# A fused attention and gated-unit block: the first four token tiles centred only, their scale applied later, and the value weights loaded in four pieces from a second queue

## The chip, the core and the metric

The kernel runs on one NeuronCore of a Trainium2 chip. The core has five engines with queues of their own: PE (TensorE, matrix products; the profile lists its weight loads as PEld), DVE (VectorE), ACT (ScalarE), POOL (GpSimd) and SP, which here only issues DMAs. Each engine works through its queue in order, and semaphores order the engines among themselves. Sixteen DMA engines move the data. The metric is the device time of one execution in microseconds, as a median over runs: before the change 222.83 us (three runs, 222.78 to 222.85). The profile was taken in another execution, of 222.43 us.

## The reference, cut to what matters

```python
xn = layernorm(x)                       # (x - mean) / sqrt(var + 1e-5), 2048 tokens x 512
out = x + A(xn) + B(xn)

def A(x):                               # 32 heads of 16
    q, k, v = split(x @ wqkv)
    phi(u) = concat(softmax(u @ w_phi), softmax(-u @ w_phi))
    kv = phi(k)^T v ;  z = sum over tokens of phi(k)
    o = (phi(q) kv) / (phi(q) z + 1e-6)
    return o @ wo

def B(x):                               # 1792 wide
    return ((x @ w_gate) * (x @ w_up)) @ w_down
```

Everything that reads the normalised tokens xn is linear in them up to the softmax, and the gated unit is a product of two such terms.

## The kernel before, in words

The 2048 tokens are 16 tiles of 128. All tensors live in one SBUF array, `arena`, so the profile's names say `arena` for nearly everything and `ps` for PSUM; the line tells the groups apart.

*Layer norm.* `emit_ln_stats` takes the statistics of a tile (L410) and aggregates them (L412) on DVE, adds epsilon (L417, on DVE for tiles 0 to 3, on POOL for the later ones) and lets POOL raise it to the power of -1/2 (L419). `emit_xn` subtracts the mean and multiplies by the root in one DVE instruction (L434). Tiles 0 to 3 go one by one; PE transposes each by four products with an identity matrix (L442), and ACT copies the result out of PSUM into `xnT` (L443). The later tiles go in groups of four, and a DMA transpose, issued by SP, turns them.

*Products.* `k_pe` makes the values of a tile (four matmuls of 512 columns with the value weights; ACT copies them out at L507). `wprime` multiplies the transposed key or query weights with a block-diagonal form of w_phi, so that one product per tile gives the input of the softmax; the four block-diagonal tiles `wbd` are made by POOL in `make_wbd` (L392) once w_phi is there. `k_pk` and `q_pk` make the softmax inputs, and `emit_exp` writes them with both signs to SBUF (two ACT instructions out of PSUM, L467 and L468), takes the maximum on DVE and lets ACT make the exponentials. `glu` is one gated unit: two groups of four matmuls, an ACT copy of the gate and a DVE product (L545). `q_num` makes numerators and denominators of the attention and divides (L614, L615). `final` adds up the down projection of the gated units and the output projection in one PSUM bank; DVE adds x (L642), and SP stores the tile.

*Order.* Nothing of the order within an engine is written out by hand. Every step is recorded with what it reads and writes, a cost, and for a DMA a time `at` before which the planner does not believe it landed. `_order` then lays the steps out greedily engine by engine: the step that can start first, by priority among equals; steps marked `urgent` may go ahead of another. The costs and the `at` times change the order in which instructions stand in the queues, and nothing else: on the chip the semaphores decide. A line of the recording helpers therefore stands for many operations (all matmuls are L297, all ACT operations L277, plain DMAs L165, DMA transposes L164).

*The beginning.* SP issues the loads of x tiles 0, 1, 2-3, the value weights in one DMA, x 4-7, the first four of fourteen column tiles of the gate and up weights, w_phi, the key weights through a DMA transpose (L361), and then the rest of the gate and up weights. PE meanwhile runs 46 matmuls on zeros (L366).

Of the kernel before, what the change touches and what calls it, by code (L numbers as in the profile page):

```python
# [197 lines left out]
def _build(nc, es, A_x, A_wqkv, A_w_phi, A_wo, B_w_gate, B_w_up, B_w_down, out):  # L198
# [93 lines left out]
    def mms(items, prio=None, warm=False):  # L292

        def fn(e):
            ins = None
            for o, l, r, a, z in items:
                ins = e.matmul(o, lhsT=l, rhs=r, start=a, stop=z)  # L297
            return ins
        reads = []
        writes = []  # L300
        c = 0.0
        for o, l, r, a, z in items:
            reads += [l, r]
            writes.append(o)
            c += max(25.0, o.free_size() / 2.4 + 2.3) * (1.6 if warm else 1.0)
        return sc.step(PE, fn, reads=reads, writes=writes, cost=c, lat=260.0, prio=prio)
# [40 lines left out]
    def load_gu(on, f0, n, at):  # L347
# [3 lines left out]

    load_x(SP, 0, 1, 3150.0)
    load_x(SP, 1, 1, 3700.0)
    load_x(SP, 2, 2, 4800.0)
    load_w(SP, wv_v, A_wqkv[:, 1024:1536].rearrange("(q p) j -> p q j", p=128), 6800.0)
    load_x(SP, 4, 4, 8200.0)
    load_gu(SP, 0, 4, 10800.0)
    sc.dma(SP, wphi_v, bass.AP(tensor=A_w_phi.tensor, offset=A_w_phi.offset, ap=[[16, 128], [2048, NQ], [1, 16]]),
           at=12500.0)
    load_wT(1, 14500.0)  # L360
    load_gu(SP, 4, 10, 20500.0)  # L361


    zero = sbv("tree", 0, 128)
    dve(lambda e: e.memset(zero, 0.0), [], [zero], 128)  # L365
    mms([(bank(7, 0, 128), zero, zero, True, True)] * 46, warm=True)  # L366

# [37 lines left out]
    pool(lambda e: e.memset(mhalf, -0.5), [], [mhalf], 4)  # L405

    def emit_ln_stats(t0, n):
        ts = slice(t0, t0 + n)
        for t in range(t0, t0 + n):
            dve(lambda e, t=t: e.bn_stats(stats_v[:, t, 0:6], x_tile(t)), [x_tile(t)], [stats_v[:, t, 0:6]], 512)  # L410
        for t in range(t0, t0 + n):
# [3 lines left out]
        rstd4 = rstd_v[:, ts, 0:1]  # L415
        add = dve if t0 < 4 else pool
        add(lambda e: e.tensor_scalar(out=veps.unsqueeze(2), in0=var4, scalar1=1e-5, scalar2=None, op0=ALU.add),  # L417
            [mv_v[:, ts, :]], [veps], n)
        pool(lambda e: e.tensor_tensor(out=rstd4, in0=veps.unsqueeze(2), in1=mhalf[:, 0:n].unsqueeze(2), op=ALU.pow),  # L419
# [8 lines left out]
    def next_a():  # L428
        b = a_bank[0] % a_banks[0]
        a_bank[0] += 1  # L430
        return b

    def emit_xn(t):
        dve(lambda e: e.tensor_scalar(out=xn_tile(t), in0=x_tile(t), scalar1=mv_v[:, t, 0:1],  # L434
                                      scalar2=rstd_v[:, t, 0:1], op0=ALU.subtract, op1=ALU.mult),
            [x_tile(t), mv_v[:, t, 0:1], rstd_v[:, t, 0:1]], [xn_tile(t)], 512, rate=0.5)
        if t >= 4:
            sc.dma(SP, xnT_v[:, :, t * 128:(t + 1) * 128], xn_tile(t), transpose=True, issue=1250.0, land=3200.0,
                   at=36000.0 + 1300.0 * (t - 8) if t >= 8 else 22500.0 + 1300.0 * (t - 4))
            return  # L440
        b = next_a()
        mms([(bank(b, q * 128, 128), xn_tile(t)[:, q * 128:(q + 1) * 128], ident, True, True) for q in range(NQ)])  # L442
        act_op(xnT_v[:, :, t * 128:(t + 1) * 128], bank(b).rearrange("p (q s) -> p q s", q=NQ))  # L443

# [15 lines left out]

    def emit_exp(src_bank, e_out):

# [3 lines left out]
        tr = (i % 2) * 1024  # L466
        act_op(pst[:, 0:512], bank(src_bank))  # L467
        act_op(pst[:, 512:1024], bank(src_bank), scale=-1.0)  # L468
        src = pst.rearrange("p (g k) -> p g k", g=16)
# [34 lines left out]
    def k_pe(t):  # L504
        b = next_a()
        mms(group(bank(b), [(xnT(q, t * 128, 128), wv_v[:, q, :]) for q in range(NQ)]))
        act_op(vext_all[:, t, :, 0:64], bank(b).rearrange("p (c j) -> p c j", c=8))  # L507

    def k_pk(t):
        b = next_a()  # L510
        mms(group(bank(b), [(xnT(q, t * 128, 128), Wp_v[:, 1, q, :]) for q in range(NQ)]))
        p_slot["k", t] = emit_exp(b, ek_v[:, t, :])

# [73 lines left out]
    def q_pk(t):  # L587
        b = next_q()
        mms(group(bank(b), [(xnT(q, t * 128, 128), Wp_v[:, 0, q, :]) for q in range(NQ)]))
        p_slot["q", t] = emit_exp(b, eq(t))  # L590

# [17 lines left out]
    def q_num(t):  # L609
# [4 lines left out]
        dve(lambda e: e.reciprocal(out=w, in_=nd[:, :, 64:68]), [nd[:, :, 64:68]], [w], 32, rate=6.0)  # L614
        dve(lambda e: e.tensor_tensor(  # L615
            out=o.rearrange("p (g h d) -> p g h d", g=8, h=4),
            in0=nd[:, :, 0:64].rearrange("p g (h d) -> p g h d", h=4),
            in1=w[:, :, :, None].to_broadcast([128, 8, 4, 16]), op=ALU.mult),
            [nd[:, :, 0:64], w], [o], 512)

# [7 lines left out]
    def final(t, b, cols=(0, 512)):  # L628
# [12 lines left out]
        xs = x_tile(t)[:, c0:c1]  # L641
        dve(lambda e: e.tensor_tensor(out=og, in0=ob, in1=xs, op=ALU.add), [ob, xs], [og], c1 - c0, prio=-2.0)  # L642
        sc.dma(SP, out_flat[t * 128:(t + 1) * 128, c0:c1], og, is_out=True)
# [21 lines left out]

    for t in range(4):
        first = len(sc.steps)
        ln(t, 1)
        for st in sc.steps[first:]:
            st.urgent = True  # L670
        k_pe(t)
    make_wbd()
    wprime(1)
    for b0 in range(0, NT, 4):
# [5 lines left out]
        if b0 == 0:  # L680
            load_later(lambda: load_x(SP, 8, 8, 29000.0))
        if b0 == 4:
# [187 lines left out]
```

## Time and profile before

| | |
|---|---|
| median of three runs | 222.83 us |
| profiled execution | 222.43 us |
| its span, first to last instruction | 220.7 us |
| PE busy | 215.4 us, 98%, 1273 matmuls |
| DVE busy | 192.8 us, 87% |
| ACT busy | 114.4 us, 52% |
| POOL busy | 9.6 us, 4% |
| HBM read, written | 8.67 MB, 2.10 MB |

The profile gives busy times of the engines, groups of instructions by line, the chain of work that ended last (followed back from the last instruction, at each step to what released it), the DMA queues, and the time from the issue of a DMA to its landing. "<-" behind an instruction names what ended the idle time before it. Times count from the first instruction of the span. The ends of matmuls are modelled, so how fast PE works is read from the distance between starts. The row PEclk is the share of the clock that a throttle granted.

### The profile page before, as it was taken

Reading aid. Unit: us, or ns where it says so; the run is one execution under the profiler, and the core shown is the slowest. Engines: PE = TensorE matmul, PEld = TensorE weight load, DVE = VectorE, ACT = ScalarE, POOL = GpSimd, SP = SyncE. Lnnn points to the kernel's source line nnn. Section 1 sums busy time; section 2 is a strip of 40 time slices with the busy share of each in tenths; the row PEclk is TensorE's granted clock in tenths of the full one; section 3 lists DMA queues with packets and bytes.
Section 4 is the critical chain, followed back from the end, with each engine's and each line's share of the span. In section 5 each row is a group of like instructions: output and inputs, shape, how many; then the busy total and the mean of one; then the engine's idle time right before and its main releaser. Section 6 shows DMA issues by size and latency. Waiting matters only on the chain.

```text
span 220.7 us, 3555 instructions
## 1 busy us (share of the span) xinstructions
PE 215.4 (98%) x1273; PEld 107.0 (48%) x1296; DVE 192.8 (87%) x552; ACT 114.4 (52%) x189; POOL 9.6 (4%) x25
## 2 busy tenths in 40 slices
PE   8899999999999999999999999999999999999995
PEld 8454444444445545444445544444445454444544
DVE  5855999999998289999999999999999999998421
ACT  2668977466442699875543676656454433230000
POOL 4250000200003000000000000000000000000000
PEclk9999999999999999999999999999999999999999
DMA  6999720139200340000000004435446556565621
GB/s 175 324 295 287 177 80 3 25 74 337 88 3 19 77 95 3 0 0 0 3 0 1 3 0 87 79 74 97 95 95 98 117 107 133 77 142 118 99 72 49
DMA packets 46386, 19.91 MB, mean 90 GB/s; under 512 B 37408, under 2 KB 45344, under 8 KB 46368
## 3 DMA queue, kind: packets, MB, share of 16 engines
q1 hardware_dynamic: 46368, 19.68, 38.5%
q8 instruction: 10, 0.16, 0.3%
q14 instruction: 8, 0.07, 0.1%
HBM read 8.67 MB, written 2.10 MB: 49 GB/s over the span
## 4 chain that ended last, share of the span: by engine, by line
PE 94%; DMA 3%; SPq 1%; issue 1%; DVE 1%
PE ps L297 94%; DMA arena<-in_A_x_dram 3%; SPq L165 1%; DVE arena L410 0%; DVE arena L434 0%; DVE arena L642 0%
## 5 line engine op out<-in xcount | busy, mean ns | idle before, releaser
L297 PE MATMUL ps<-arena 128*128 128x512 bf16 (+4 forms) x1273 | 215.4, 331 | 3.0 <-DVE arena L365 1.0
L297 PEld LDWEIGHTS ps<-arena 128*128 128x128 bf16 x1296 | 107.0, 100 | 111.2 <-ACT arena L277 2.2
L277 ACT ACTIVATE arena<-ps 128x512 bf16<-128x512 f32 (+1 forms) x156 | 83.2, 596 | 53.2 <-PE ps L297 45.3
L277 ACT ACTIVATE arena<-arena 128x1024 bf16<-128x1024 bf16 x32 | 34.3, 1082 | 28.2 <-DVE arena L480 25.9
L494 DVE TENSOR_TENSOR arena<-arena 128x512 f32<-128x512 bf16 (+3 forms) x128 | 48.8, 393 | 0.1
L545 DVE TENSOR_TENSOR arena<-ps,arena 128x512 bf16<-128x512 f32 x56 | 38.0, 679 | 3.9 <-ACT arena L277 2.2
L474 DVE TENSOR_TENSOR arena<-arena 128x512 bf16<-128x512 bf16 (+3 forms) x128 | 31.6, 269 | 4.6 <-ACT arena L277 4.4
L480 DVE TENSOR_TENSOR arena<-arena 128x1024 bf16<-128x1024 bf16 x32 | 21.5, 673 | 0.0
L642 DVE TENSOR_TENSOR arena<-ps,arena 128x512 bf16<-128x512 f32 (+2 forms) x17 | 11.1, 651 | 7.4 <-PE ps L297 7.2
L410 DVE BATCH_NORM_STATS2 arena<-arena 128x6 f32<-128x512 bf16 x16 | 10.7, 681 | 1.5 <-DMA arena<-in_A_x_dram 1.5
L521 DVE TENSOR_TENSOR arena<-arena 128x1024 bf16<-128x1024 bf16 x16 | 10.9, 680 | 0.0
L615 DVE TENSOR_TENSOR arena<-ps,arena 128x512 bf16<-128x512 f32 x16 | 10.8, 673 | 0.1
L614 DVE RECIPROCAL arena<-ps 128x32 f32<-128x32 f32 x16 | 5.6, 348 | 3.7 <-PE ps L297 3.5
L518 DVE RECIPROCAL arena<-arena 128x64 bf16<-128x64 f32 x16 | 8.6, 539 | 0.0
L434 DVE TENSOR_SCALAR arena<-arena 128x512 bf16<-128x512 bf16 x16 | 6.1, 406 | 2.2 <-issue 1.5
L601 DVE TENSOR_TENSOR arena<-arena 128x512 bf16<-128x512 bf16 x16 | 6.5, 407 | 0.0
L419 POOL TENSOR_TENSOR arena<-arena 128x1 f32<-128x1 f32 (+1 forms) x7 | 5.3, 764 | 4.1 <-DVE arena L417 3.8
L598 DVE RECIPROCAL arena<-arena 128x32 f32<-128x32 f32 x16 | 5.4, 336 | 0.0
L417 POOL TENSOR_SCALAR arena<-arena 128x4 f32<-128x4 f32 x3 | 1.1, 380 | 55.1 <-DVE arena L412 55.1
L599 DVE TENSOR_TENSOR arena<-arena 128x32 bf16<-128x32 f32 x16 | 2.7, 171 | 0.0
L412 DVE BATCH_NORM_AGGREGATE arena<-arena 128x2 f32<-128x6 f32 x16 | 2.0, 160 | 0.1
L561 DVE TENSOR_TENSOR arena<-ps,arena 128x65 f32<-128x65 f32 x8 | 1.6, 220 | 0.4 <-PE ps L297 0.4
(19 smaller groups left out, 9.8 us busy)
## 6 DMA issues: line engine op xcount, KB each, us to landing
out_dram<-arena SPq DMA_DIRECT2D x15, 128.0 KB, 2.0
arena<-in_B_w_down_dram SPq DMA_DIRECT2D x1, 1792.0 KB, 7.5
arena<-in_B_w_gate_dram SPq DMA_DIRECT2D x1, 1280.0 KB, 6.8
arena<-in_B_w_up_dram SPq DMA_DIRECT2D x1, 1280.0 KB, 10.3
arena<-in_A_x_dram SPq DMA_DIRECT2D x1, 1024.0 KB, 5.4
arena<-arena SPq DMA_TRANSPOSE x44, 2.8
arena<-in_A_wqkv_dram SPq DMA_DIRECT2D x1, 512.0 KB, 4.2
arena<-in_A_x_dram SPq DMA_DIRECT2D x1, 512.0 KB, 5.7
```

The lines of the kernel that those rows point to most:

```text
L277: return e.activation(out=out_ap, in_=in_ap, func=func, scale=scale, **kw)
L297: ins = e.matmul(o, lhsT=l, rhs=r, start=a, stop=z)
L410: dve(lambda e, t=t: e.bn_stats(stats_v[:, t, 0:6], x_tile(t)), [x_tile(t)], [stats_v[:, t, 0:6]], 512)
L474: dve(lambda e, dst=dst, src=src, k=k: e.tensor_tensor(out=dst, in0=src[:, :, 0:k], in1=src[:, :, k:2 * k], op=ALU.max), [src], [dst], 16 ...
L480: dve(lambda e: e.tensor_tensor(out=p4, in0=p4, in1=src[:, :, None, :].to_broadcast([128, 16, 16, 4]), op=ALU.subtract), [pst, src], [pst] ...
L494: dve(lambda e, dst=dst, src=src, k=k: e.tensor_tensor(out=dst, in0=src[:, :, 0:k], in1=src[:, :, k:2 * k], op=ALU.add), [src[:, :, 0:2 * ...
L518: dve(lambda e: e.reciprocal(out=rs, in_=sm), [sm], [rs], 64, rate=6.0)
L521: dve(lambda e: e.tensor_tensor(out=e4, in0=e4, in1=r4[:, :, None, :].to_broadcast([128, 16, 16, 4]), op=ALU.mult), [ek_v[:, t, :], rs], [ ...
L545: dve(lambda e: e.tensor_tensor(out=dst, in0=bank(bu), in1=gr, op=ALU.mult), [bank(bu), gr], [dst], 512, prio=-1.0)
L601: dve(lambda e: e.tensor_tensor(out=e1, in0=e1, in1=rs[:, :, None, :].to_broadcast([128, 8, 16, 4]), op=ALU.mult), [e1, rs], [e1], 512, ra ...
L615: dve(lambda e: e.tensor_tensor(out=o.rearrange("p (g h d) -> p g h d", g=8, h=4), in0=nd[:, :, 0:64].rearrange("p g (h d) -> p g h d", h= ...
L642: dve(lambda e: e.tensor_tensor(out=og, in0=ob, in1=xs, op=ALU.add), [ob, xs], [og], c1 - c0, prio=-2.0)
```

## The change

Five things change together.

1. *Tiles 0 to 3 are only centred.* DVE takes statistics, aggregates and subtracts the mean; the transposes and all products of these tiles work on the unscaled tile. The root of variance and epsilon is made by POOL beside that (two instructions for each tile).
2. *The scale comes later.* Values and softmax inputs of these tiles are multiplied by the root as ACT takes them out of PSUM (an operand with one value for each token); the negative half of the softmax input is then made from the positive half in SBUF, and no longer from PSUM. The gated units stay unscaled, which leaves the square of the scale to be made good: the attention's quotient is multiplied by variance plus epsilon, and the final addition of x multiplies the whole sum by its reciprocal. Both are fused into the DVE instruction that was there (`scalar_tensor_tensor` for `tensor_tensor`). One DVE instruction makes the four reciprocals.
3. *Loads.* The four x tiles are loaded one by one from SP; the value weights come in four pieces of 128 rows that ACT issues. On SP the first gate and up weights now stand ahead of x 4-7; w_phi and the key weights follow as before.
4. *PE.* 28 matmuls on zeros instead of 46, and three more behind the transpose of tile 0. That transpose comes in two halves with an ACT copy each, and tile 0's value product in two steps of two matmuls.
5. *The planner's numbers.* The `at` times of the loads and transposes and the cost of the matmuls on zeros are others.

```diff
-    load_x(SP, 0, 1, 3150.0)
-    load_x(SP, 1, 1, 3700.0)
-    load_x(SP, 2, 2, 4800.0)
-    load_w(SP, wv_v, A_wqkv[:, 1024:1536].rearrange("(q p) j -> p q j", p=128), 6800.0)
-    load_x(SP, 4, 4, 8200.0)
-    load_gu(SP, 0, 4, 10800.0)
+    for t in range(4):
+        load_x(SP, t, 1, 3100.0 + 500.0 * t)
+        load_w(ACT, wv_v[:, t, :], A_wqkv[t * 128:(t + 1) * 128, 1024:1536], 3400.0 + 550.0 * t)
+    load_gu(SP, 0, 4, 8000.0)
+    load_x(SP, 4, 4, 9600.0)
...
-           at=12500.0)
-    load_wT(1, 14500.0)
-    load_gu(SP, 4, 10, 20500.0)
+           at=9900.0)
+    load_wT(1, 11900.0)
+    load_gu(SP, 4, 10, 19500.0)
...
-    mms([(bank(7, 0, 128), zero, zero, True, True)] * 46, warm=True)
+    mms([(bank(7, 0, 128), zero, zero, True, True)] * 28, warm=True)
...
+    RAW = 4
+    def emit_centred(t):
+        dve(lambda e: e.bn_stats(stats_v[:, t, 0:6], x_tile(t)), [x_tile(t)], [stats_v[:, t, 0:6]], 512)
+        dve(lambda e: e.bn_aggr(mv_v[:, t, :], stats_v[:, t, 0:6]), [stats_v[:, t, 0:6]], [mv_v[:, t, :]], 6)
+        dve(lambda e: e.tensor_scalar(out=xn_tile(t), in0=x_tile(t), scalar1=mv_v[:, t, 0:1], scalar2=None,
+                                      op0=ALU.subtract), [x_tile(t), mv_v[:, t, 0:1]], [xn_tile(t)], 512, rate=0.5)
...
+    def emit_root(t):
+        pool(lambda e: e.tensor_scalar(out=veps(t), in0=mv_v[:, t, 1:2], scalar1=1e-5, scalar2=None, op0=ALU.add),
+             [mv_v[:, t, :]], [veps(t)], 1)
+        pool(lambda e: e.tensor_tensor(out=rstd_v[:, t, 0:1], in0=veps(t), in1=mhalf[:, 0:1], op=ALU.pow),
+             [veps(t), mhalf], [rstd_v[:, t, 0:1]], 1, rate=155.0, fixed=400.0)
+    def emit_squares():
+        dve(lambda e: e.reciprocal(out=lnt_v[:, 2, 0:RAW], in_=lnt_v[:, 0, 0:RAW]), [lnt_v[:, 0, 0:RAW]],
+            [lnt_v[:, 2, 0:RAW]], RAW, rate=6.0)
+    def scale_of(t):
+        return rstd_v[:, t, 0:1] if t < RAW else 1.0
...
+    def emit_T(t, parts=1):
+        n = NQ // parts
+        for q0 in range(0, NQ, n):
+            b = next_a()
+            mms([(bank(b, q * 128, 128), xn_tile(t)[:, q * 128:(q + 1) * 128], ident, True, True)
+                 for q in range(q0, q0 + n)])
+            act_op(xnT_v[:, q0:q0 + n, t * 128:(t + 1) * 128],
+                   bank(b, q0 * 128, n * 128).rearrange("p (q s) -> p q s", q=n))
...
-        act_op(pst[:, 0:512], bank(src_bank))
-        act_op(pst[:, 512:1024], bank(src_bank), scale=-1.0)
+        act_op(pst[:, 0:512], bank(src_bank), scale=scale_of(t))
+        act_op(pst[:, 512:1024], bank(src_bank) if t >= RAW else pst[:, 0:512], scale=-1.0)
...
+        if t < RAW:
+            dve(lambda e: e.scalar_tensor_tensor(out=o4, in0=n4, scalar=veps(t), in1=w4, op0=ALU.mult, op1=ALU.mult),
+                [nd[:, :, 0:64], veps(t), w], [o], 512)
+            return
...
+            r2 = lnt_v[:, 2, t:t + 1]
+            dve(lambda e: e.scalar_tensor_tensor(out=og, in0=ob, scalar=r2, in1=xs, op0=ALU.mult, op1=ALU.add),
+                [ob, r2, xs], [og], c1 - c0, prio=-2.0)
...
-    for t in range(4):
+    for t in range(RAW):
         first = len(sc.steps)
-        ln(t, 1)
+        emit_centred(t)
+        emit_T(t, 2 if t == 0 else 1)
         for st in sc.steps[first:]:
             st.urgent = True
+        if t == 0:
+            mms([(bank(7, 0, 128), zero, zero, True, True)] * 3, warm=True).deps.append(sc.by_eng[PE][-2])
+        emit_root(t)
         k_pe(t)
     make_wbd()
+    emit_squares()
     wprime(1)
```

## The prediction

> **What bounds the kernel now.** I read the shares of the chain that ended last first, then that chain in order of time.
>
> ```profile
> PE 94%; DMA 3%; SPq 1%; issue 1%; DVE 1%
> ...
> PE ps L297 94%; DMA arena<-in_A_x_dram 3%; SPq L165 1%; DVE arena L410 0%; DVE arena L434 0%; DVE arena L642 0%
> ```
>
> ```profile
> 2.70 5.72 DMA arena<-in_A_x_dram
> 8.42 0.02 issue
> 8.44 0.69 DVE arena L410
> 9.14 0.33 DVE arena L434
> 9.46 0.05 issue
> 9.51 6.47 PE ps L297 x44
> ...
> 206.54 11.92 PE ps L297 x79
> 218.45 0.02 issue
> 218.48 0.29 DVE arena L642
> ```
>
> From 9.51 us PE runs without a stop to 218.44. Its matmuls of 512 columns start every 0.216 us, those of 128 every 0.056; the only wait I find on the way is about 0.18 us at 155.6. So the end moves only if PE gets through its first 15 us sooner or later, or if PE gains a stop. What holds the 9.51: x tiles 4 to 7 land at 8.42, DVE's queue has their first statistics (L410) ahead of the normalisation of tile 3 (L434), and PE's transpose of tile 3 waits for that.
>
> The next gate is further down PE's queue: wprime (16 matmuls of 128 columns from 14.92). It needs the transposed key weights (a DMA transpose) and the four wbd tiles from POOL (L392), which need w_phi. The DMA view, asked for the stretch in which both are under way, and POOL's timeline:
>
> ```profile
> arena<-in_A_w_phi_dram SPq DMA_DIRECT2D x1, 16.0 KB, 7.3
> arena<-in_A_wqkv_dram SPq DMA_TRANSPOSE x1, 8.3
> ```
>
> ```profile
> 11.61 0.23 POOL L417 TENSOR_SCALAR arena<-arena 128x4 f32<-128x4 f32 x1 [3.42 <-DVE arena L412]
> 11.92 1.05 POOL L419 TENSOR_TENSOR arena<-arena 128x4 f32<-128x4 f32 x1
> 12.93 1.83 POOL L392 TENSOR_TENSOR arena<-arena 128x128 bf16<-128x128 bf16 x4
> ```
>
> Issued at 4.35 and 5.11, they land at 11.61 and 13.39. The wbd tiles are done at 14.76, and PE comes at 14.92: wprime is already nearly late. Both transfers stand behind 2.62 MB (x 0-7, value weights, the first gate and up weights), so I ask for the DMA's rate in stretches (columns: length, PE busy (count), clock, DMA share, GB/s).
>
> ```profile
> 1.75:2.25 0.50, 0.50 (x8) 1.00 0.59 170
> 2.25:2.75 0.50, 0.50 (x8) 1.00 0.97 273
> 2.75:3.00 0.25, 0.25 (x5) 1.00 1.46 230
> 3.00:3.50 0.50, 0.50 (x8) 1.00 0.77 109
> ...
> 4.25:4.50 0.25, 0.25 (x5) 1.00 1.01 205
> ...
> 5.00:9.75 4.75, 3.97 (x35) 1.00 1.06 359
> ```
>
> At 359 GB/s the 2.62 MB would take 7.30 us from the first packet (1.84). In the packets the engines come to the end of them at 10.15 on average (8.31 us: 1.01 us lost on all of them, nearly all before 5 us), the slowest at 10.81 (0.66 more). The weight transpose moves only when the slowest is through: its packets stand until 11.34.
>
> **The change, part by part.** *Queue positions.* The instruct order of both kernels: PE had 46 warm-up matmuls, now 28 and 3; tile 0's transpose is in two halves, and its value matmul in two pairs around tile 1's transpose; after tile 3's transpose PE has 16 matmuls of 512 columns (values of tiles 2 and 3, one gated unit) before wprime, where it had 24 (two units). The rest of PE's real work is the same.
>
> *Normalisation.* For tiles 0 to 3 DVE no longer does the add of epsilon (L417, 4 x 0.15 us, now POOL's) and no longer waits for POOL's root (L419, 0.56 us each), and their whole chain stands ahead of tile 4's statistics. One tile then costs 0.72 (statistics to aggregate) + 0.22 (to the next dependent one, 3.65 to 3.87) + 0.30 (L434 at 4.75 to L417 at 5.05) = 1.24 us. x tile 0 landed at 2.90 and started DVE at 2.92. It now shares the engines with the first value piece: between 0 and 0.37 us later (131 KB at 359 GB/s); I take 0.25, the two rings taking turns. Tile 3's centring ends at 3.17 + 3 x 1.24 + 0.94 + 0.38 = 8.21, and PE's transpose of tile 3 starts at 8.3 instead of 9.51, if PE is free. PE's own chain there (transpose 0 at 4.55, eviction, values of tile 0 at 5.7, transposes at 6.1 and 7.0, values of tile 1 to 8.35) just fits.
>
> *PE reaches wprime* at 8.3 + 4 x 0.056 + 16 x 0.216 = 12.0, against 14.92, of which 8 x 0.216 = 1.73 us is the unit put behind it. With nothing in the way the end moves by 14.92 - 12.0 - 1.73 = 1.19 us.
>
> *But wprime waits.* w_phi keeps its place behind the same 2.62 MB. Call D the time by which the slowest engine is through earlier. w_phi lands at 11.61 - D; POOL, whose roots are done by 9, starts 0.08 later (11.53 to 11.61 in its row above), needs 1.83 for the four wbd tiles, and PE follows 0.16 later (14.76 to 14.92): 13.68 - D. The weights (13.39 - D) come before that. The end moves by 14.92 - 1.73 - (13.68 - D) = **0.49 us later, less D**. While PE waits there, everything behind it stands, the gated units too; nothing else hides it.
>
> *D* is what the value pieces on ACT's queue can bring; no row shows two queues. Lower end: the load of x 8-15, one large DMA, also ran at 68 to 190 GB/s for its first 1.5 us, though nothing delayed its issue; then a start is slow by itself, and D is 0. Upper end: the loss on all engines and the lag of the slowest go, 1.01 + 0.66 = 1.67 us. I take 1.0, since it is nearest to the row of 359 GB/s, in which several DMAs stand queued, as they now do from the first microsecond: eight pieces of 131 KB on two queues, and an engine whose piece on one queue is not ready has the other. The lag I leave as it is. Then the end moves by 0.49 - 1.0 = -0.51 us.
>
> [...]
>
> *What is late next.* Tile 4's value matmul waited for its DMA transpose (landed 22.66, used at 22.72). It now stands 9.54 us of matmuls behind wprime's start, so at 23.22 - D; the transposes stand behind the large gate and up loads and come at 22.66 - D, if those move up too. If not, D = 1 costs 22.66 - 22.22 = 0.44 there.
>
> *Costs I put at nothing.* ACT issues four DMAs (SP's took 0.40 to 0.51 us each) before its table load of 1.28 us: ready at 4.1, first eviction at 4.9; without that 0.8 us each lateness is PE's. Twelve evictions with a scale by row and eight negations out of SBUF: a 512 out of PSUM took 0.60, 1024 out of SBUF 1.08, so 0 to 0.5 us each, 10 in all at most, on an engine busy 52%; behind them stand evictions that free PE's banks, and only in 20 to 24 us was ACT full. Eight fused operations at L615 and L642: between the plain ones (0.65 to 0.67) and the sum with an operation of 0.22 (L568), so 0 to 1.8 us on DVE, which from 80 to 200 us is busy 118.4 of 120; I take 0, it is the same stream of 512 elements. The q transposes landed 0.4 to 1 us before PE used them; a DVE later by more would stop PE by the rest. The reciprocal (0.16 to 0.34) replaces 0.6 us of adds.
>
> **Rivals.**
> 1. *The second queue saves issue only.* Idle shares of the engines before 5 us (1.06 less the row's share, by length, from 1.84) add up to 0.46 us; that is then all of D: +0.03, 222.86 us. For it: the slow start of x 8-15. Against: packets of 0.3 to 0.6 us at 2.8 to 3.7, where one DMA follows another.
> 2. *The DMAs hold nothing up.* D reaches 1.67, PE arrives unhindered: -1.19, 221.64. For it: the lag of the slowest engine is one of two or three, and may go with the order. Against: it arose at 6.4 to 8.4, where one queue was full.
> [...]
> 4. *D is 0 or below* (two queues in each other's way): 0.49 or more later, 223.32.
>
> **How the numbers follow.** The profiled execution took 222.43 us (span 220.7 and 1.73 around it), 0.40 under the median of 222.83; differences are carried over to the median. Forecast: 222.83 - 0.51 = 222.32, so **222.3**. Chances: forecast (D 0.7 to 1.4) 0.45; rival 2 0.2; rival 1 (D 0.1 to 0.7, or the 0.44 of tile 4) 0.2; rivals 3 and 4 0.15 together. A change under 0.2% (0.45 us) is about what a measurement of this kernel can't tell from none. Faster by more needs D over 0.94: 0.30 of the forecast's 0.45 and rival 2, 0.5. Slower by more: rivals 3 and 4 where they are not a little milder, 0.13. The rest, 0.37, is within. Range: 221.6 (rival 2) to 223.3 (rival 4's bound).
>
> **What would show it.** Right: the transpose of tile 3 at 8.3; w_phi at 10.6 and the weights at 12.4; PE standing some 0.7 us before wprime, which starts at 12.7; tile 4's matmul without a stop. Rival 1: w_phi at 11.1. Rival 2: wprime at 12.0, no stand. [...] A stop of PE after 30 us would be outside all of this, and would make the prediction wrong.

## The result

The kernel after takes 223.71 us (median of 22 runs, 223.19 to 224.01), the kernel before on the same chips 222.68 (22 runs). The ratio is 1.0039, with a 95% interval of 1.0029 to 1.0050: **slower by about 0.9 us** (the medians differ by 1.03). 222.3 had been predicted, within 221.6 to 223.3.

The profiled executions differ by 1.33 us (223.76 against 222.43). PE ends at 219.11 instead of 218.44, which is 0.67. The other 0.66 lies behind PE: from its end to the end of the execution 4.65 us pass instead of 3.99. The two profiles lie further apart than the medians, since that of before was taken in an execution 0.25 us under its median.

The shares of the chain that ended last:

```profile
PE 93%; DMA 2%; DVE 1%; ACT 1%; issue 1%; SPq 0%; POOL 0%
```

The same chain in order of time (start, length, what). Before, it ran from x 4-7 over DVE to PE at 9.51 and then on PE alone:

```profile
1.71 4.64 DMA arena<-in_A_x_dram
...
6.38 0.70 DVE arena L410
...
7.67 0.61 DVE arena L410
...
8.58 0.42 POOL arena L419
...
9.03 0.60 ACT arena L277
...
9.66 0.39 PE ps L297
...
10.66 0.60 ACT arena L277
...
11.31 6.28 PE ps L297 x40
```

PE now works without a stop from 11.31, not from 9.51. The chain begins with x tile 2, which DVE waited for until 6.35 (before, x 2 and 3 had landed at 4.66), and passes through DVE, POOL and ACT to the values of tiles 1 to 3. Tile 3's transpose starts at 9.88, not at 8.3. The line of 6.28 us runs over wprime, which starts at 13.95. PE came there at 13.91, so the chain shows no wait. POOL's timeline, and the DMA view of the stretch in which both transfers are issued, show how close the gate was (the last column is us from issue to landing):

```profile
11.97 1.83 POOL L391 TENSOR_TENSOR arena<-arena 128x128 bf16<-128x128 bf16 x4 [2.32 <-DMA arena<-in_A_w_phi_dram]
```

```profile
arena<-in_A_w_phi_dram SPq DMA_DIRECT2D x1, 16.0 KB, 7.6
arena<-in_A_wqkv_dram SPq DMA_TRANSPOSE x1, 8.3
```

w_phi lands at 11.83 (before 11.61), the wbd tiles are done at 13.80, the key weights land at 13.46 (13.39). **Two gates meet at wprime**: PE's own arrival at 13.91, and POOL's tiles at 13.80. Where PE stood waiting for these tiles, it followed 0.14 to 0.15 us behind them (13.89 to 14.03 with 46 warm-ups, 15.30 to 15.45 with eight loads on one queue), so POOL's gate opened at about 13.95, within 0.04 of PE's arrival. With a unit of 1.73 us put behind it, wprime had to start by 14.92 - 1.73 = 13.19, the break-even, for the end not to move; it starts 0.76 later, and from there to PE's end only 0.1 us are lost (at 144.1; before 0.18 at 155.6).

The loads in two stretches (length, then busy time and count of PE, PEld, DVE, ACT and POOL, clock, DMA share, GB/s):

```profile
1.75:5.00 3.25, 2.61 (x26) 2.35 (x24) 1.72 (x5) 1.28 (x1) 0.80 (x5) 1.00 0.93 261
5.00:9.75 4.75, 4.48 (x22) 2.36 (x22) 3.55 (x11) 2.43 (x5) 3.44 (x7) 1.00 1.06 350
```

Before, the two stretches moved 240 and 359 GB/s. The second queue brought 21 GB/s for 3.25 us, 0.07 MB, and lost 0.04 MB in the stretch behind. The mean hides what happened inside the first stretch. In three parts, for PE alone (columns: length, PE busy (count), clock, DMA share, GB/s), first before, then after:

```profile
1.75:2.50 0.75, 0.75 (x10) 1.00 0.77 223
2.50:4.00 1.50, 1.50 (x17) 1.00 0.95 219
4.00:5.50 1.50, 1.50 (x17) 1.00 0.99 309
```

```profile
1.75:2.50 0.75, 0.75 (x10) 1.00 0.69 97
2.50:4.00 1.50, 1.50 (x17) 1.00 1.06 354
4.00:5.50 1.50, 0.86 (x9) 1.00 0.89 254
```

For 1.5 us the two queues do reach the rate that the prediction hoped for. They start with less, and fall back from 4.00 on.

The tail, in the DMA view from 218.3 us on, first after:

```profile
q14 instruction: 1, 0.01, 0.6%
...
out_dram<-arena SPq DMA_DIRECT2D x1, 32.0 KB, 2.1
```

and before:

```profile
out_dram<-arena SPq DMA_DIRECT2D x1, 32.0 KB, 1.4
```

The last store took 2.06 us from issue to landing, before 1.44. A block of instructions of 8 KB was read at 220.40, among the store's packets (220.34 to 220.86). Before, that block came at 220.47, behind the store's landing at 220.24.

### The profile page after: what moved, and what is told of

It reads as the page before. It is cut to its first block, busy times and chain, and to the rows that moved or that the text cites. A ratio compares the mean times of both kernels' runs of the same rounds, so it can differ in the third digit from the quotient of the medians.

```text
span 222.0 us, 3543 instructions
## 1 busy us (share of the span) xinstructions
PE 215.8 (97%) x1257; PEld 105.9 (48%) x1281; DVE 193.0 (87%) x549; ACT 116.4 (52%) x190; POOL 11.1 (5%) x29
## 4 chain that ended last, share of the span: by engine, by line
PE 93%; DMA 2%; DVE 1%; ACT 1%; issue 1%; SPq 0%; POOL 0%
PE ps L297 93%; DMA arena<-in_A_x_dram 2%; ACT arena L277 1%; DVE arena L410 1%; SPq L165 0%; POOL arena L419 0%; DVE arena L411 0%; DVE arena L412 0%; DVE arena L682 0%
## 5 line engine op out<-in xcount | busy, mean ns | idle before, releaser
L297 PE MATMUL ps<-arena 128*128 128x512 bf16 (+3 forms) x1257 | 215.8, 332 | 3.3 <-DVE arena L364 1.0
L277 ACT ACTIVATE arena<-ps 128x512 bf16<-128x512 f32 (+2 forms) x137 | 72.6, 587 | 44.6 <-PE ps L297 39.3
L277 ACT ACTIVATE arena<-arena 128x1024 bf16<-128x1024 bf16 (+1 forms) x40 | 38.7, 978 | 29.4 <-DVE arena L510 29.2
L577 DVE TENSOR_TENSOR arena<-ps,arena 128x512 bf16<-128x512 f32 x56 | 38.1, 680 | 2.6 <-PE ps L297 2.3
L504 DVE TENSOR_TENSOR arena<-arena 128x64 bf16<-128x64 bf16 (+3 forms) x128 | 32.1, 272 | 4.7 <-ACT arena L277 4.3
L682 DVE TENSOR_TENSOR arena<-ps,arena 128x512 bf16<-128x512 f32 (+2 forms) x13 | 8.4, 647 | 7.4 <-PE ps L297 7.2
L277 ACT ACTIVATE arena<-ps,arena 128x512 bf16<-128x512 f32 x12 | 8.0, 682 | 5.4 <-PE ps L297 4.9
L654 DVE TENSOR_TENSOR arena<-ps,arena 128x512 bf16<-128x512 f32 x12 | 8.2, 683 | 0.1
L466 DVE TENSOR_SCALAR arena<-arena 128x512 bf16<-128x512 bf16 x12 | 4.2, 407 | 1.7 <-POOL arena L442 1.7
L440 POOL TENSOR_SCALAR arena<-arena 128x4 f32<-128x4 f32 x3 | 0.8, 258 | 51.7 <-DVE arena L436 51.7
L442 POOL TENSOR_TENSOR arena<-arena 128x4 f32<-128x4 f32 x3 | 3.3, 1095 | 0.2
L679 DVE SCALAR_TENSOR_TENSOR arena<-ps,arena 128x512 bf16<-128x512 f32 x4 | 3.0, 746 | 0.0
```

The source lines that it names most:

```text
L277: return e.activation(out=out_ap, in_=in_ap, func=func, scale=scale, **kw)
L504: dve(lambda e, dst=dst, src=src, k=k: e.tensor_tensor(out=dst, in0=src[:, :, 0:k], in1=src[:, :, k:2 * k], op=ALU.max), [src], [dst], 16 ...
L577: dve(lambda e: e.tensor_tensor(out=dst, in0=bank(bu), in1=gr, op=ALU.mult), [bank(bu), gr], [dst], 512, prio=-1.0)
L654: dve(lambda e: e.tensor_tensor(out=o4, in0=n4, in1=w4, op=ALU.mult), [nd[:, :, 0:64], w], [o], 512)
```

## The experiments

Theory A: the two gates at wprime set PE's end, and removing one leaves the other. Rivals: B, the cold PE alone (a PE that still works at half pace, 0.43 us for a matmul of 512 columns); C, the second queue alone. Theory T concerns the tail: the place of the block of instructions makes it long. All runs stood beside the kernel before on the same chip, with a median of 222.55 to 222.69. The table gives, from each profiled execution, the start of tile 3's transpose (T3), of wprime, the end of PE, and the rest up to the end of the execution; then the median of 4 to 12 runs (22 in the first two rows) and its ratio to before. All in us.

| kernel | T3 | wprime | PE end | rest | median | ratio (95%) |
|---|---|---|---|---|---|---|
| before | 9.51 | 14.92 | 218.44 | 3.99 | 222.68 | |
| after | 9.88 | 13.95 | 219.11 | 4.65 | 223.71 | 1.0039 (1.0029 to 1.0050) |
| values from SP | 11.07 | 15.10 | 220.27 | 4.02 | 224.28 | 1.0069 (1.0042 to 1.0096) |
| 46 warm-ups | 8.90 | 14.03 | 219.20 | 4.40 | 223.58 | 1.0041 (1.0027 to 1.0055) |
| w_phi early | 8.38 | 13.35 | 218.53 | 4.42 | 223.65 | 1.0042 (1.0026 to 1.0058) |
| both of these | 8.54 | 15.56 | 220.74 | 4.49 | 223.52 | 1.0051 (1.0029 to 1.0074) |
| before, values on ACT | 12.45 | 18.11 | 221.64 | 4.01 | 226.60 | 1.0144 (1.0104 to 1.0184) |
| late scale alone, 28 | 9.30 | 15.69 | 219.21 | 4.95 | 225.33 | 1.0089 (1.0053 to 1.0126) |
| late scale alone, 46 | 9.15 | 15.54 | 219.11 | 5.04 | 224.23 | 1.0059 (1.0034 to 1.0085) |
| true landings | 9.14 | 13.81 | 218.24 | 4.42 | 222.85 | 1.0002 (0.9979 to 1.0024) |
| after, w_down in two | 10.19 | 14.22 | 219.40 | 4.06 | 223.41 | 1.0045 (1.0017 to 1.0072) |
| true landings, w_down in two | 9.13 | 13.91 | 218.41 | 4.07 | 222.50 | 0.9995 (0.9984 to 1.0007) |
| one queue, eight in turn | 8.62 | 15.45 | 219.88 | 4.04 | 223.92 | 1.0078 (1.0047 to 1.0109) |
| wprime later | 10.06 | 16.69 | 221.26 | 5.11 | 226.36 | 1.0173 (1.0149 to 1.0197) |
| one queue, pairs | 8.80 | 14.11 | 218.55 | 4.01 | 223.01 | 1.0014 (0.9999 to 1.0029) |
| two queues, pairs | 9.38 | 14.05 | 218.49 | 4.00 | 222.75 | 1.0007 (0.9991 to 1.0022) |

PE's end and the rest add up to the time of the profiled execution, and five of these lie 0.45 us or more off their kernel's median: below it by 0.70 (w_phi early), 1.17 (late scale alone, 28), 0.95 (before, values on ACT) and 0.45 (one queue, pairs), above it by 1.71 (both of these). What such a trace shows is true of its execution, and need not be of the median.

**The value weights from SP's queue, in one DMA behind x 3.**

```diff
-        load_w(ACT, wv_v[:, t, :], A_wqkv[t * 128:(t + 1) * 128, 1024:1536], 3400.0 + 550.0 * t)
+    load_w(SP, wv_v, A_wqkv[:, 1024:1536].rearrange("(q p) j -> p q j", p=128), 5050.0)
```

> The changed kernel, with the value weights loaded by one DMA from SP behind x tile 3; every engine's other instructions stand in the same order. Theory A (two gates meet at wprime: PE arrives at 13.9 us, the wbd tiles are done at 13.8, and whichever is later sets the end): x tiles 2 and 3 land by 5.5 instead of 6.35 and 7.07, w_phi at about 11.6 and the weights at 13.4, but PE stays cold until about 9.5, so that wprime starts at 13.6 to 13.9 instead of 13.95: 0 to 0.3 us faster than the changed kernel, still 0.4 to 0.8 slower than before. Theory B (the cold PE alone sets the end): no change against the changed kernel. Theory C (the second queue holds up two DMA engines and that alone costs the time): x tiles as in A, and 0.6 us or more of the loss goes.

224.28 is slower than after, which none of the three theories had. x 2 and 3 landed at 3.92 and 4.42, in after at 6.35 and 7.07; the values at 7.09; w_phi at 11.92 and the key weights at 13.57, each within 0.11 of after. So the value pieces do hold up the x tiles, and with one queue or two the same bytes are through at the same time. The chain shows what was late instead:

```profile
2.64 4.45 DMA arena<-in_A_wqkv_dram
7.09 0.14 issue
7.23 3.38 PE ps L297 x14
```

PE waited for the values until 7.23, and took 3.38 us for what follows, at half pace. The profile's PEclk fell too (columns as above; the last three are clock, DMA share, GB/s):

```profile
7.50:10.80 3.30, 3.10 (x14) 1.68 (x14) 0.62 (x4) 1.77 (x3) 0.98 (x2) 0.50 1.12 335
```

The trace's record of the clock has the full clock from 4.05 and half from 7.46 to 10.87: PE had been idle for most of 4.1 to 7.4 (0.83 us busy of 3.30).

**46 warm-ups instead of 28**, in the same order.

```diff
-    mms([(bank(7, 0, 128), zero, zero, True, True)] * 28, warm=True)
+    mms([(bank(7, 0, 128), zero, zero, True, True)] * 46, warm=True).cost *= 28 / 46
```

> The changed kernel with 46 matmuls on zeros again instead of 28, all else in the same order. PE should be at full pace from about 6.4 us instead of 9.5. Theory A: PE then arrives at wprime at 12.7 to 13.2 and stands until the wbd tiles are done at 13.8: wprime again at 13.9, the end moves by less than 0.1 us. Theory B: the arrival sets it; wprime at 13.0 and 0.8 to 1.0 us faster than the changed kernel, at or below the kernel before. Theory C: no change.

Full pace came at 4.2 instead of 9.5, tile 3's transpose 0.98 earlier, and PE at wprime at 12.93. There it stood, as its waits between 12 and 16.5 us show (total, times, longest; a wait counts from the modelled end of the matmul before it, so it is shorter than the 1.1 us from 12.93 to 14.03):

```profile
PE ps L297 <- POOL arena L391: 0.9, 1, 0.9
```

wprime at 14.03, PE's end 219.20 against 219.11: one gate removed, nothing gained. Theory B, which had 0.8 to 1.0 us for this, falls.

**w_phi ahead of the first gate and up weights and x 4-7 on SP's queue.**

```diff
-    load_gu(SP, 0, 4, 8000.0)
-    load_x(SP, 4, 4, 9600.0)
...
+    load_gu(SP, 0, 4, 8000.0)
+    load_x(SP, 4, 4, 9600.0)
```

> The changed kernel with the DMA of w_phi issued ahead of the first gate and up weights; all other orders are the same. w_phi should land by 8, the wbd tiles be done at about 11.5 us. Theory A: alone it brings nothing, since PE arrives at 13.9: less than 0.1 us. Theory B: nothing. Rival to both (w_phi alone is the gate): 0.4 us faster, limited by the key weights at 13.46.

The key weights' transpose stays where it was. w_phi landed at 6.64, the wbd tiles were done at 10.99. PE, in this execution at full pace from 5.6 by itself, came at 12.3 and stood for the third of wprime's conditions, the key weights:

```profile
PE ps L297 <- DMA arena<-in_A_wqkv_dram: 0.9, 1, 0.9
```

The key weights landed at 13.30. PE's end, 218.53, is 0.58 better than after, and still behind before. This was the fastest of six runs, with the cold PE gone by luck. The median, 223.65, is that of after, as theory A has it for this edit alone.

**Both edits.**

> Both: 46 matmuls on zeros and w_phi early. Theory A: PE arrives at 12.7 to 13.2, the wbd tiles are ready at 11.5, and the key weights (landed 13.46) are now last: wprime at 13.55, 0.4 us faster than the changed kernel, though neither part alone brought 0.1. Theory B: as much as 46 warm-ups alone, 0.8 to 1.0. Theory C: nothing.

Theory A had 0.4 us less than after, and that did not come: the median, 223.52, tells it from neither edit alone. The profile doesn't say why. It caught the slowest of nine runs, in which fifteen of the sixteen parts of the key weights' landing were there by 14.04 and the last at 15.52, so that PE stood 3.1 us. Why both edits together bring nothing in the median stays open. The key weights are at least the last gate of the three: in no kernel with the first gate and up weights ahead of them did they land before 12.99.

**The second queue alone, in the kernel before.**

```diff
-    load_w(SP, wv_v, A_wqkv[:, 1024:1536].rearrange("(q p) j -> p q j", p=128), 6800.0)
+    for t in range(4):
+        load_w(ACT, wv_v[:, t, :], A_wqkv[t * 128:(t + 1) * 128, 1024:1536], 6800.0)
```

> The kernel before, with nothing changed but its value weights: four pieces from ACT's queue instead of one DMA from SP's. Order of PE's and DVE's work as before. This measures D (what the second queue brings) in the frame of before. Theory A (the second queue brings nothing, D is 0 or a little below): x 4-7 land at 8.4 to 8.7 as before (8.42), w_phi and the key weights within 0.2 us of before, the transpose of tile 3 at 9.5 to 9.8, the time 222.7 to 223.0. The forecast's D of 1.0: x 4-7 at 7.4, w_phi at 10.6, the transpose of tile 3 at about 8.6, 221.9. Theory C (the second queue alone costs all of the loss): 223.5.

All three figures missed: 226.60. x 4-7 landed at 9.10 (before 8.42), w_phi at 12.41: D is -0.7 to -0.8 here. The value pieces went ahead of x 2-3, which landed at 7.29 instead of 4.66, and the chain starts there:

```profile
1.71 5.58 DMA arena<-in_A_x_dram
7.32 0.70 DVE arena L411
```

PE, busy for 2.14 of the 3.30 us from 4.1 to 7.4, was cold afterwards too (its clock at half from 8.81 to 12.22), and tile 3's transpose slipped by 2.9 us.

**The late scale alone, with the loads and planner's numbers of before**, once with 28 and once with 46 warm-ups (the difference to before is parts 1, 2 and 4 of the change, with or without the cut from 46 to 28).

> The kernel after, with the loads of before (value weights in one DMA from SP's queue, x 2-3 together, the planner's landing times of before); 28 warm-ups. By these times the planner puts five groups of four gated matmuls ahead of wprime instead of two. The break-even of wprime is then 14.92 + 4 x 0.216 = 15.78 us, far behind its gates (key weights 13.4, wbd by 14.8 at the latest), so only the start of the chain counts. Theory A (the loss lay in the late x tiles and in the place of wprime, not in the late scaling): the transpose of tile 3 at 8.3 to 8.7 where the full pace comes by 7, wprime at 14.6 to 14.9, 0.86 us earlier than before, 221.8. Theory B (a cold PE alone): with only 28 warm-ups the full pace may come after 9; then the transpose of tile 3 at 9.3 to 9.6, 222.5 to 222.8. If the late scaling itself costs (fused operations on DVE, scaled evictions on ACT), 223 or more, with new stops of PE after 24 us.

> The same as the late scaling alone, with 46 warm-ups as in before instead of 28, in the same order of work. Theory A: full pace by 6.5, the transpose of tile 3 at 8.3 to 8.7, wprime at 14.6 to 14.9, the transposes of tile 4 (landed 22.66 in before) used at 22.7: 0.6 to 0.9 us earlier than before, 221.8 to 222.1. Theory B: 0.5 us better than the kernel with 28 warm-ups. If the late scaling itself costs: 223 or more.

225.33 and 224.23. By the time, and by new stops of PE, both runs meet the third expectation, that the late scaling itself costs. The trace of the second points elsewhere. DVE is as early as the forecast had it, and PE is not. DVE's timeline, the last centring:

```profile
7.49 0.35 DVE L413 TENSOR_SCALAR arena<-arena 128x512 bf16<-128x512 bf16 x1
```

and the chain:

```profile
2.18 4.66 DMA arena<-in_A_wqkv_dram
7.19 1.90 PE ps L297 x11
9.15 7.45 PE ps L297 x48
```

Tile 3 is ready at 7.84, but the value weights land at 6.84, and PE has six value matmuls and tile 2's transpose ahead of tile 3's: 9.15. With DVE off the path, **the value weights' landing is the next gate**. PE lost time a second time: wprime at 15.54 was 0.24 ahead of its break-even there (15.78), yet PE's end was 0.67 later than before. Between the starts of matmuls, 1.0 to 1.3 us are lost at 138.5, 142.9, 143.3, 146.7 and 160.7, waits for DVE and ACT that the kernel after doesn't have. The planner's order from there on is another one; the fused operations are in both, and they are also in the kernel of 222.50 further down, which equals before. So the late scaling alone doesn't cost this, and the order is what differs; what of the order costs it was not taken apart. Of the 1.72 us by which this profiled execution is slower than that of before, 1.05 lie behind PE. Why the two medians are 1.1 us apart is open too: the two profiled executions, 224.16 and 224.15, both had PE at full pace before 6.

**The kernel after, the planner told the landings that after's trace shows, 46 warm-ups.** wprime then stands behind 20 matmuls after tile 3's transpose, not 16 (break-even 14.05).

```diff
-    for t in range(4):
-        load_x(SP, t, 1, 3100.0 + 500.0 * t)
+    for t, (ax, aw) in enumerate(((3500.0, 3700.0), (4050.0, 4250.0), (6100.0, 6400.0), (7000.0, 7250.0))):
+        load_x(SP, t, 1, ax)
...
-    load_gu(SP, 0, 4, 8000.0)
-    load_x(SP, 4, 4, 9600.0)
+    load_gu(SP, 0, 4, 10100.0)
+    load_x(SP, 4, 4, 11700.0)
...
-           at=9900.0)
-    load_wT(1, 11900.0)
+           at=11900.0)
+    load_wT(1, 13600.0)
```

> The kernel after, its loads on two queues unchanged, but the planner is told the landing times that the trace of after shows, and PE has 46 warm-ups. The order that comes out has three groups of four gated matmuls ahead of wprime instead of two, and one more group ahead of tile 4's value matmul. Break-even of wprime is 14.92 - 4 x 0.216 = 14.05 us. Theory A (two gates meet at wprime, and a later place for it brings back what was lost): the transpose of tile 3 at 8.9, PE reaches wprime at 13.4, the gates hold it until 13.9, so 0.1 us earlier than before at PE's end: 222.5 to 222.8. If the second queue costs something else (theory C), the time stays at 223.5.

Broadly as theory A has it: wprime at 13.81, PE's end 218.24, 0.20 better than before and 0.87 better than after, 222.85 in all. The expected wait at wprime didn't occur, since w_phi landed at 11.39 in this execution and tile 3's transpose came at 9.14, not at 8.9. Theory C, which had 223.5 for this kernel with its second queue, falls. PE's end is better than before and the time is not: that is the tail, 4.42.

**The tail: w_down's load, at some 55 us, in two DMAs.** SP issues one DMA more; nothing else changes its order. Once on after, once on the kernel with true landings.

```diff
-            load_later(lambda: load_w(SP, wd_v, B_w_down.rearrange("(f p) j -> p f j", p=128), 48000.0),
+            load_later(lambda: load_w(SP, wd_v[:, 0:7, :], B_w_down[0:896, :].rearrange("(f p) j -> p f j", p=128), 48000.0),
+                       lambda: load_w(SP, wd_v[:, 7:14, :], B_w_down[896:1792, :].rearrange("(f p) j -> p f j", p=128), 48000.0),
```

> The kernel after, with one edit far from the start: w_down's load at about 55 us in two DMAs instead of one, so SP has one instruction group more. The order of PE, DVE, ACT and POOL is the same. In after's trace an 8 KB packet of instructions was read at 220.40 us, among the last store's packets (220.34 to 220.86), and that store landed 2.06 us after its issue (before: 1.44, the instruction packet at 220.47 behind it). In the kernel with the values from one SP DMA, which also has one SP DMA more, the packet came at 218.78 and the store took the short time. Theory T (the instruction packet delays the last store, and SP's instruction count places it): the packet comes 1 us or more before the last store's packets, the store lands 1.4 us after its issue, PE's end stays at 219.1, the time 223.1 to 223.3, 0.4 to 0.6 us below after. If the tail has another cause: 223.7 and a landing of 2.0 us.

> The kernel with the planner told the true landings (222.85), with w_down's load in two DMAs. Theory T: PE's end at 218.2 as there, the last store 0.4 us sooner, 222.4: 0.1% faster than before. If the tail has another cause: 222.85.

The block of instructions came at 217.66 and 216.65, and the last store (DMA view of the first of the two, from 218.3 on; no line for q14 is left) took

```profile
q1 hardware_dynamic: 288, 0.13, 12.5%
...
out_dram<-arena SPq DMA_DIRECT2D x1, 32.0 KB, 1.5
```

The rest behind PE fell from 4.65 to 4.06 and from 4.42 to 4.07. In the median the second fell from 222.85 to 222.50, as expected; the first from 223.71 to 223.41, with PE's end 0.29 later in its profiled execution (cold until 10). In both pairs the intervals of the ratios overlap, so the times alone don't settle it. The traces do more: all sixteen kernels sort themselves: where that block was read between 0.2 us ahead of the last store's first packet and its last, the rest is 4.40 to 5.11; where it came 2.3 us or more ahead, or 0.4 or more behind the last packet, 3.99 to 4.07.

**The eight pieces in turn, all from SP's queue** (x 0, piece 0, x 1, ...), otherwise the kernel with true landings.

```diff
-        load_w(ACT, wv_v[:, t, :], A_wqkv[t * 128:(t + 1) * 128, 1024:1536], aw)
+        load_w(SP, wv_v[:, t, :], A_wqkv[t * 128:(t + 1) * 128, 1024:1536], aw)
```

> The kernel with the planner told the true landings (222.85), with the four value pieces on SP's queue too, in turn with the x tiles (x 0, piece 0, x 1, piece 1, ...). The order of all work but SP's and ACT's issues is the same. It separates the second queue from the order of the eight pieces. If the second queue brings nothing of its own (rival 1 and theory A: D is 0): x 0 earlier by 0.5 us, the last of the eight pieces within 0.4 us of 6.67, w_phi within 0.3 of 11.4, the time 222.6 to 223.1. If two queues do carry the pieces sooner: the last piece at 7.3 or later (SP needs 0.4 to 0.5 us for each issue), the transpose of tile 3 at 9.7, 223.4. If two queues hinder each other (theory C): the last piece at 6.2, w_phi 0.5 us sooner, 222.3.

The last piece landed at 6.85 (two queues: 6.67), but the gate weights behind them were issued 1.9 us later, at 4.54, and w_phi landed at 13.33 (11.39). PE stood 1.9 us at wprime. Neither theory had such a late w_phi. The second queue was worth as much here as its four pieces cost SP in issue, 0.46 to 0.48 us each. That the issues are the cause is read from this equality alone: behind them, from 5.00 to 9.75, the rate was lower as well, 276 GB/s against 358.

**wprime later, in after**, by two of the planner's numbers.

```diff
-           at=9900.0)
-    load_wT(1, 11900.0)
+           at=11900.0)
+    load_wT(1, 13900.0)
```

> The kernel after, with two of the planner's numbers changed: w_phi and the key weights are expected 2 us later (11.9 and 13.9, near their landings). wprime then stands behind 24 matmuls of 512 columns after tile 3's transpose, as in before, instead of 16; 28 warm-ups and both queues as in after. So its gates (13.8) are far from binding, and only PE's own arrival counts. Break-even 14.92. Theory A (in after PE's arrival, 13.91, and the gates, 13.8, met, and both have to go): PE arrives at 13.91 + 8 x 0.216 = 15.64, 0.72 after the break-even, as in after: 223.4 to 223.9. If the gates at wprime alone made the loss: 222.7 to 223.0.

The trace has wprime behind 28 matmuls of 512 columns after tile 3's transpose (starts from 10.29 to 16.47), not behind 24, so its break-even is 14.92 + 4 x 0.216 = 15.78. PE came at 16.68 and started wprime without a wait, 0.9 behind the break-even; theory A had 0.72. But at 226.36 the time is far from both expectations, and the run doesn't decide between them: the order changed elsewhere as well. POOL's timeline, for one, has the root of tiles 4 to 7 (L440, L442) between the wbd tiles:

```profile
14.50 0.40 POOL L391 TENSOR_TENSOR arena<-arena 128x128 bf16<-128x128 bf16 x1
14.85 1.05 POOL L442 TENSOR_TENSOR arena<-arena 128x4 f32<-128x4 f32 x1
15.87 0.40 POOL L391 TENSOR_TENSOR arena<-arena 128x128 bf16<-128x128 bf16 x1
```

The last of these tiles was done at 16.27, still ahead of PE. Later stops of 2.0 us were added (1.0 of it for a DMA transpose at 173.7), and the rest behind PE is 5.11.

**The same bytes in five DMAs**, on one queue (x 0, x 1, values 0-1, x 2-3, values 2-3) and on two (three x from SP, two value DMAs from ACT), in the order and with the tail of the kernel of 222.50.

> The kernel with true landings and w_down in two (222.50), with the first 1.05 MB from SP's queue alone in five DMAs: x 0, x 1, value pieces 0 and 1 in one, x 2 and 3 in one, pieces 2 and 3 in one. No second queue; the order of PE's work is the same. If the second queue is needed only because eight pieces take SP eight issues (rival 1): with five issues the last value bytes land by 6.8, w_phi and the key weights within 0.3 us of two queues (11.75, 13.39), the transpose of tile 3 at 8.6 to 9.1, wprime at 13.5 to 13.9, 222.0 to 222.5: no worse than with two queues. If two queues do carry more (the forecast's D): w_phi 0.5 us or more later, wprime after 14.3, 223.0 or more.

> The same with two queues: the x tiles in three DMAs from SP's, the value weights in two from ACT's (w_down in three DMAs, so that SP issues as many in all as with w_down in two). If the bytes of the first 1.05 MB bound the start in whatever queue they stand (theory A): the last value bytes at 6.4 to 7.0, x 2 and 3 only 0.3 us before them, the transpose of tile 3 at 9.0 to 9.3, w_phi within 0.3 us of the kernel with one queue, 222.3 to 222.7. If coarser DMAs on two queues lose less time: the values by 6.0, the transpose of tile 3 at 8.4, w_phi at 11.2, 222.0.

One queue: last values 7.07, w_phi 11.99, key weights 13.63, T3 8.80, then 0.6 us of waiting at wprime. Two: last values 6.05 but x 2-3 at 6.25, w_phi 11.51, key weights 13.12, T3 9.38, no wait at wprime. The two PE ends are 0.06 apart. Neither pair of expectations is met: w_phi lies 0.48 apart, where theory A had at most 0.3, and on one queue wprime at 14.11 lies between the two expectations, while the median of 223.01 is where the forecast's D would have put it. The intervals of the two ratios overlap, so the two kernels can't be told apart by time. With the first 1.05 MB in at most six DMAs on SP's queue, w_phi landed at 11.61 to 11.99 (before, late scale twice, values from SP, one queue in pairs); on two queues, with the order of after's loads, at 11.39 to 11.92 (seven kernels). So D lies between -0.3 and 0.2, about as far from one execution to the next as from one queue to two. No version beat before: the best, 222.50 beside 222.55, is its equal.

## Why the prediction was wrong

**Two steps failed. The first is D, taken as 1.0**: the time by which the slowest DMA engine is through earlier, read from w_phi's landing. It measured -0.22 (w_phi 11.83). Put into the prediction's own sum, 14.92 - 1.73 - (13.68 + 0.22), it gives an end 0.71 later; PE's end moved by 0.67. The mechanism (wprime waits for w_phi, the unit put behind it sets the break-even) was right, and so was the rival with D at or below 0, 223.32. The value was chosen because it was nearest to the row of 359 GB/s, on the ground that several DMAs then stand queued. From 2.50 to 4.00 the two queues did reach 354 GB/s (301 to 354 in all ten kernels with value pieces on ACT's queue, 219 to 253 in the six without). But up to 2.50 they moved 97 against 223, and from 4.00 to 5.50 254 against 309, so the mean before 5 us stayed at 261. Why they start with less and fall back was not taken apart. In every kernel but one (before with the values on ACT, 7.94) the last of the first 1.05 MB, x 0-3 and the values, came between 6.2 and 7.3, whatever the queue: D near 0, the lower end that the prediction had named. What the second queue saved, as far as the runs show, was time of issue: with all eight DMAs on one queue, four issues more took SP 1.9 us, and w_phi came at 13.33 against 11.39.

**The second is PE's arrival at wprime, forecast for 12.0**: it came at 13.91, 0.72 behind the break-even of 13.19. That alone would have made PE's end about as late, had D been 1.0. The run with 46 warm-ups has the arrival at 12.93, and there POOL's gate held. The lateness starts at tile 3's transpose.

*Tile 3's transpose at 8.3* came at 9.88. 0.67 came from DVE: x 0 was 0.57 later than before, not 0.25, and x 2 was not there when DVE had done tile 1 (centring of tile 3 ended at 8.88, not 8.21). The other 0.9 came from PE, whose own chain "just fits" only with the value pieces there at 5.7 and at full pace: piece 3 landed at 7.26, and until 9.5 a matmul of 512 columns took 0.427 us. Behind the transpose PE lost another 0.34 before 11.31, where it waited for ACT's copy of tile 3; the prediction had no time for that.

*Rival 3, the cold PE,* was true as well, and by itself cost nothing: PE came at 13.91, where POOL's gate opened at 13.95 anyway. The prediction gave it and rival 4 one chance, 0.15 together, as alternatives; they are gates of one instruction, and both held. With 46 warm-ups full pace came by 6.5 in all ten kernels that have them (in one, before with the values on ACT, it was lost again from 8.81 on); with 28 it came at 5.4, 5.6, 9.5, 10 and 10, and once, early, was lost again. The stretch at half clock was 3.41 us long with the values from SP (7.46 to 10.87), and as long in before with the values on ACT (8.81 to 12.22); no run shows what sets its length or the time of full pace.

*Costs put at nothing.* A scaled eviction took 0.682 us (0.613 without), a fused DVE operation 0.746 (0.683), so 0.8 us on ACT and 0.5 on DVE; with 0.1 us of stops in 30 to 219, that they are hidden held. Tile 4's matmul found its transpose landed (23.21, used at 23.47). ACT's first eviction was not delayed by its four issues: the table load behind them was over at 3.96, and the eviction came at 5.28, when PE was done.

*The tail* was in no step. The prediction took what lies behind PE as fixed; it grew by 0.66 in the profiled execution, as much as PE's lateness. Two runs move the block of instructions away with one DMA more on SP, and the rest falls to that of before; all sixteen kernels agree on where the block lies when the rest is long. That the block itself holds up the store, and not something that goes with its place, is inferred from that. Which engine reads it, and why the added work of the change put it there, the trace doesn't say. That SP's count of instructions moves it speaks for SP.

The loss is thus two gates that meet at wprime, 0.67 in the profiled executions, and a longer tail, 0.66, which goes with a block of instructions; in the medians both make 0.9. Taken away together (true landings, 46 warm-ups, w_down in two) they leave a kernel equal to before: the late scaling takes DVE off the path, and the landing of the x tiles and value weights, at 6.2 to 7.3 us, takes its place.

## What to carry to other kernels

Before an early chain is shortened, list what else its end waits for, and price the next gate of each engine: three of them (PE's arrival, w_phi, the key weights) stood here within 0.5 us. Don't count on a second issuing queue for more bytes: here it saved time of issue (1.9 us for four issues), and the value pieces that it put in front delayed the x tiles (x 2 and 3 at 6.35 and 7.07, against 3.92 and 4.42 without). And compare the time behind the last matmul, too: here one DMA more at 55 us went with an end that was 0.35 to 0.6 us shorter, as much as the edits under test were worth.

## What was not expected of the hardware

- A block of 8 KB of instructions, read within 0.2 us ahead of or among the packets of the last store, went with an end that was 0.4 to 0.65 us longer (4.40 to 4.65 against 3.99 to 4.07; 4.95 to 5.11 in three kernels whose last stores are also issued at other times), though the packet itself took only 0.31 to 0.60 us of one DMA engine.
- The granted clock in the window rows stayed at 1.00 in after while matmuls of 512 columns started every 0.427 us until 9.5; in the kernel with the values from SP it showed 0.50 at the same pace. The trace of after holds no record of the clock at all, that of before none ahead of 6.53, and the view prints 1.00 where there is none. The pace between starts is the surer sign.
- Packets of the key weights' DMA transpose had begun by 10.0 and then stood. The first of these went on 0.5 us after the end of the last packet of the 2.6 MB ahead of them (11.46 after 10.97 in after; 11.33 after 10.81 before), and the transpose landed 2.0 us later (13.46 and 13.39).
